# Four GpSimd scalings of the output weight behind the last normalised tile, and the stores of tiles 9 to 13 behind their adds

## The chip, the core and the metric

The kernel runs on one core of a Trainium2 chip. The core has five instruction streams that work side by side and meet only where one waits for another's semaphore: TensorE (PE, with its weight loads shown as PEld), VectorE (DVE), ScalarE (ACT), GpSimd (POOL) and SyncE (SP), which issues nearly all DMAs. The metric is device time in microseconds (us) of one execution, the median of the runs shown.

## The reference

A linear-attention mixer and a gated MLP with spatial mixing, both with adaptive layer norm from a condition vector `c`. S = 2048 rows, D = 448, 16 heads of 28, Fh = 896; all inputs are bfloat16.

```python
sa, ca, ga, sb, cb, gb = (silu(c) @ w_mod).reshape(6, -1)
h = layernorm(x) * (1 + ca) + sa
q, k, v = h @ wqkv                         # per head
phi(t) = [softmax(t @ w_phi), softmax(-t @ w_phi)]
o = (phi(q) @ (phi(k).T @ v)) / (phi(q) @ sum(phi(k)) + 1e-6)
x = x + ga * (o @ wo)
h = layernorm(x) * (1 + cb) + sb
z = gelu(h @ w_in)
z1, z2 = z[:, :Fh], layernorm(z[:, Fh:])
g = w_sp @ z2 + b_sp                       # mixes the 2048 rows
x = x + gb * ((z1 * g) @ w_out)
```

The last line is the one that the change concerns. The kernel folds `gb` into the weight: it multiplies each row block of `w_out` by `gb` once (and `wo` by `ga`), so that the product is already gated.

## The kernel before

All work is cut into tiles of 128 rows of x, numbered 0 to 15. A long string named `ORDER` (lines 482 to 525) lists every step in the order in which it is recorded, and `fast_path` (line 528) walks through it. A word such as `kP:13/G` calls the step `kP` for tile 13 on GpSimd; `/V` is VectorE, `/S` ScalarE, `/Y` SyncE; `@A0` names the PSUM bank that a matmul step writes. No scheduler moves anything afterwards: each engine executes its own instructions in the order of the string, and waits where an operand or a bank is not ready.

The stages overlap, but they come in this order. **Keys and values** (`kM`, `vM`, `kE`, `kF`, `kS`, `kR`, `kP`, `kA`): for every tile, exponentials of the key features, their sums, their normalised form (`kP`, line 873, tile `f_phik`, on VectorE or GpSimd), and an accumulation over all tiles in one bank, `kvacc`. **The joint**: when tile 15 is accumulated, `KV` and `KZ` copy `kvacc` into `f_KVbd`, and only then can the first products with the queries start. **Queries and output of the attention** (`qM`, `nM`, `nX`, `nC`, `nS`, `nT`, `nA`, `T2`, `wM`/`wN`, `wR`): `qM` (line 907) multiplies four tiles by the query weight, `qE` and `qF` exponentiate into `f_Eq`, `nM` (line 935, tile `num`) multiplies by `f_KVbd`. For a pair of tiles `nX` (ScalarE, `f_Sx`) and `nC` (VectorE, `f_cr`) prepare the denominators, `nS` is three VectorE instructions (line 950 a sum into `f_dn`, line 951 a reciprocal, line 952 a product into `f_w`), `nT` (line 955) scales a tile's numerators out of PSUM into `f_t` and so frees its bank, `nA` (line 961) adds the two halves into `f_opad` on VectorE or GpSimd, `T2` (line 834) transposes `f_opad` into `f_oT` by DMA, and `wN` (lines 969 and 971, `x_ps`) multiplies by `wo`. In between, `SHw` and `SCw` (lines 766 and 768 to 774) shift and scale the MLP's input weight `f_win`; `SCw:3,1/G` and `SCw:1,1/G` are two scalings on GpSimd that wait for `SHw:3` and `SHw:2`.

**Normalised z2** (`zM`, `zG`, `zQ`, `zR`, `zW`, `zN`) and **z1** (`yM`, `yG`) are made per tile; `zN` (line 1037, tile `f_z2n`) of tile 14 runs on GpSimd, that of tile 15 on VectorE. **Spatial mixing** (`gM`, line 1059, tile `g_ps`) multiplies `w_sp` by all sixteen tiles of `f_z2n`; `gG` (lines 1065 and 1066) adds `b_sp` and multiplies by z1. **Output** (`oM`, line 1072, `o_ps`) multiplies by `w_out`, `oE` (line 1075) adds x, and `oD` (line 1094) stores the tile. Tile 15 is done in two column parts, 256 and 192 wide: `oN` (line 1083), `oF` (line 1087), `oG` (line 1091), part 0 stored from SyncE's queue and part 1 from ScalarE's.

The two kinds of scaling that matter here share line 924: `wos:k` multiplies block k of `f_wo`, `wts:k` block k of `f_wout` (seven blocks), both 128 x 448 or 112 x 448 in bfloat16 with both inputs in SBUF. Before, `wts:4` runs early, `wts:3` late (both on GpSimd), `wts:5` on VectorE, and `wts:0`, `wts:6`, `wts:2` and `wts:1` stand on GpSimd between `kP:13` and the joint, mixed with `wos:1` to `wos:3`.

On SyncE's queue each store waits for its add; whatever stands behind it waits with it. After the last store every engine takes one branch (line 1161, to a general path that these inputs do not need) and then meets the others at the end (line 1189).

Of the kernel before, what the change touches and what calls it, by code (L numbers as in the profile page):

```python
# [498 lines left out]
T2:0,1 W:0,6 nT:1 SCw:3,1/G SCw:1,1/G SCw:0,2/V SCw:0,3/V SCw:2,1/V nA:1/G T2:1,2 qE:3 qM:4@A2 qM:5@A1 qF:4 qE:4 nM:2@A0 nM:3@A2 nX:2 nC:2 nX:3 nC:3
nS:1 qF:5 nT:2 nT:3 qE:5 wN:0@B0 wR:0/S SHw:1@B1 nM:4@A1 nM:5@A0 SCw:0,1/S nX:4 nX:5 nC:4 nC:5 nS:2 nA:2/G nT:4 nA:3/G nT:5 nA:4/G wN:1@B0 wQ:0/S  # L500
wR:1/S wQ:1/S SHw:0@B1 SCw:2,0/S l2R:0,2/G l2r:0,2 l2a:0/G SCw:0,0/V nA:5/V T2:2,4 T2:4,6 qM:6@A2 nM:6@A1 nM:7@A0 wN:2@B0 wN:3@B1 qE:6 nX:6 nC:6 nX:7
nC:7 nS:3 nT:6 nT:7 qF:6 wR:2/S wQ:2/S wR:3/S wQ:3/S l2R:2,4/V nA:6/G nA:7/G l2r:2,4 l2a:3/G l2a:2/G qM:7@A2 nM:8@A1 nM:9@A0 wN:4@B0 wM:5@B1 W:1,1
T3:0,1 T2:6,8 qE:7 nX:9 nC:9 nX:8 qF:7 zM:0@A2 wR:4/S gt zG:0 nC:8 l2a:1/V nS:4 nT:8 nT:9 T3:1,2 wR:5/V nM:10@A1 nX:10 wM:6@B0 wQ:4/V wR:6/V SCw:1,0/G
SCw:3,0/G wQ:5/S l2R:4,6/G l2r:4,6 l2a:4/G nM:11@A0 nX:11 nC:10 nC:11 zQ:0/S zM:1@A2 zG:1 zQ:1/S zR:0,2/G zW:0,2 nA:8/V nS:5 nA:9/V nT:10 T3:2,4
wM:7@B0 wR:7/V l2a:5/V W:1,5 T2:8,10 T3:4,6 yM:0,0@B1 zM:2@A2 zM:3@A1 yG:0,0 wQ:6/S zG:2 zG:3 nT:11 nM:12@A0 nM:13@A2 wQ:7/V zN:0/V zN:1/V nX:12
wM:8@B0 wM:9@B1 nC:12 nX:13 nC:13 zQ:3/S zQ:2/S zM:4@A1 nA:10/V nS:6 wR:8/V nA:11/G nT:12 nT:13 wR:9/V nA:12/V nA:13/V l2R:6,8/G l2r:6,8 l2a:6/G
l2a:7/G T2:10,12 wQ:8/S wQ:9/V zR:2,4/G zW:2,4 yM:0,1@B0 l2R:8,10/G l2r:8,10 l2a:8/G l2a:9/G zG:4 yG:0,1 zQ:4/S zN:2/V zN:3/V zM:5@A0 nM:14@A2
nM:15@A1 wN:10@B0 wN:11@B1 zG:5 nX:14 nX:15 nC:14 nC:15 nS:7 wR:10/S wQ:10/V nT:14 nT:15 nA:14/V nA:15/V wR:11/S zQ:5/S zR:4,6/G zW:4,6 T3:6,8 zM:6@A0
zG:6 wQ:11/S zQ:6/S T2:12,14 W:1,0 wM:12@B0 wM:13@B1 zM:7@A2 l2R:10,12/V yM:0,4@A1 yM:1,4@A0 l2r:10,12 l2a:11/G T3:8,10 T2:14,16 zG:7 zQ:7/S zN:4/V
zN:5/V zR:6,8/G zW:6,8 wR:13/V yG:0,4 wQ:13/S zM:8@A2 zM:9@A1 l2a:10/V wR:12/V wM:14@B0 wM:15@B1 wQ:12/V l2R:12,14/V W:1,3 T3:10,12 W:2,1 l2r:12,14  # L510
l2a:12/G zN:6/V zN:7/V yG:1,4 zG:8 zG:9 zQ:8/S W:1,4 zM:10@A2 zM:11@A1 zQ:9/S zR:8,10/G zW:8,10 zG:10 zG:11 zQ:11/S wR:14/V l2a:13/V T3:12,14 W:2,3
W:2,7 wR:15/V wQ:14/V wQ:15/V l2R:14,16/V yM:1,2@B0 zM:12@A2 zM:13@A1 yG:1,2 zG:12 yM:1,3@B0 yM:0,2@B1 yM:2,1@A2 yM:2,5@A0 zQ:10/V zN:8/V zN:9/V
zR:10,12/V l2r:14,16 l2a:14/V l2a:15/V zG:13 zQ:13/S zW:10,12 T3:14,16 W:1,2 zN:10/V zN:11/V zQ:12/V W:2,0 W:2,6 W:1,7 W:2,5 W:2,4 W:2,2 yG:1,3 yG:2,1
zM:14@A1 zM:15@A2 yG:2,5 W:1,6 zG:14 zG:15 zQ:15/S yM:1,5@B0 yG:0,2 yM:3,0@A1 yM:0,6@A2 yM:1,1@A0 yG:3,0 yG:1,1 yG:1,5 wts:3/G zR:12,14/V zW:12,14
# [679 lines left out]
```

## Time and profile before

| | us |
|---|---|
| runs: median of 3 | 263.35 |
| runs: lowest, highest | 263.28, 263.9 |
| the profiled execution's own time | 262.58 |
| its span, first instruction to last | 260.8 |
| PE busy in the span | 251.4 |
| DVE busy | 158.8 |
| ACT busy | 108.1 |
| POOL busy | 88.7 |

The profile is of one execution. Its span starts at 0 with the first instruction; 1.8 us of the execution's own time lie outside of it. Views that the text uses: the page's engine sums; busy time by stretches; the chain of waits, which is followed back from the last instruction; the timeline of an engine, where a row gives start, length, engine, line, operation, output<-inputs, how many instructions are merged in it, and in brackets how long the engine stood idle before and what ended that; and the rows of one source line. An engine's name with a q (SPq, ACTq) is its queue of instructions that issue, wait or branch. Names such as `f_win` are tiles.

### The profile page before, as it was taken

Reading aid. Unit: us, or ns where it says so; the run is one execution under the profiler, and the core shown is the slowest. Engines: PE = TensorE matmul, PEld = TensorE weight load, DVE = VectorE, ACT = ScalarE, POOL = GpSimd, SP = SyncE. Lnnn points to the kernel's source line nnn. Section 1 sums busy time; section 2 is a strip of 40 time slices with the busy share of each in tenths; the row PEclk is TensorE's granted clock in tenths of the full one; section 3 lists DMA queues with packets and bytes.
Section 4 is the critical chain, followed back from the end, with each engine's and each line's share of the span. In section 5 each row is a group of like instructions: output and inputs, shape, how many; then the busy total and the mean of one; then the engine's idle time right before and its main releaser. Section 6 shows DMA issues by size and latency. Waiting matters only on the chain.

```text
span 260.8 us, 4348 instructions
## 1 busy us (share of the span) xinstructions
PE 251.4 (96%) x1634; PEld 135.3 (52%) x1643; DVE 158.8 (61%) x358; ACT 108.1 (41%) x224; POOL 88.7 (34%) x149
## 2 busy tenths in 40 slices
PE   7999999999899999999999999999999999999992
PEld 5745655664555554444444444444444444566691
DVE  4899999869999998883005242422570283306762
ACT  3898977645899889887610400200000000000000
POOL 6419896994588887643200000000000000000000
PEclk9999999999999999999999999999999999999999
DMA  7996969993376566969600000002009700030012
GB/s 173 275 296 129 216 131 222 234 221 63 58 125 120 105 129 132 180 125 182 120 0 3 1 0 0 20 11 67 0 3 172 127 0 3 18 106 0 3 38 64
DMA packets 68799, 25.23 MB, mean 97 GB/s; under 512 B 58273, under 2 KB 68642, under 8 KB 68770
## 3 DMA queue, kind: packets, MB, share of 16 engines
q1 hardware_dynamic: 68160, 24.40, 45.6%
q10 hardware_dynamic: 610, 0.47, 0.6%
q8 instruction: 15, 0.25, 0.4%
q14 instruction: 14, 0.11, 0.2%
HBM read 8.87 MB, written 1.84 MB: 41 GB/s over the span
## 4 chain that ended last, share of the span: by engine, by line
PE 84%; DVE 9%; DMA 2%; ACT 2%; issue 1%; POOL 1%; SPq 0%; ACTq 0%; DVEq 0%
PE g_ps L1059 37%; PE z_ps L1015 9%; PE z_ps L1043 9%; PE o_ps L1072 8%; PE x_ps L971 4%; PE v_ps L860 3%; PE q_ps L907 3%; PE k_ps L852 3%; DVE f_t L955 2%; PE kvacc L883 2%; DMA f_wk_raw<-in_A_wqkv_dram 2%; PE num L935 2%; DVE f_ksum L866 2%; DVE f_phik L873 1%; PE sh_ps L761 1%
## 5 line engine op out<-in xcount | busy, mean ns | idle before, releaser
L1059 PEld LDWEIGHTS <-f_z2n 128*128 128x128 bf16 x560 | 50.1, 98 | 47.0
L1065 DVE TENSOR_TENSOR f_gb<-g_ps,f_bsp 128x512 f32<-128x512 f32 (+2 forms) x35 | 20.4, 582 | 55.9 <-PE g_ps L1059 53.7
L1059 PE MATMUL g_ps<-f_Eq,f_z2n 128*128 128x512 bf16 x218 | 49.0, 379 | 0.3
L1046 ACT ACTIVATE f_z1T<-z_ps 128x512 bf16<-128x512 f32 x28 | 15.6, 592 | 61.8 <-PE z_ps L1043 61.7
L1015 PE MATMUL z_ps<-f_win,f_hT 112*128 112x448 bf16 (+1 forms) x128 | 26.2, 352 | 0.2 <-ACT f_z2g L1019 0.2
L1043 PE MATMUL z_ps<-f_hT,f_win 113*128 113x512 bf16 (+1 forms) x112 | 26.1, 379 | 0.0
L1059 PE MATMUL g_ps<-f_hT,f_z2n 128*128 128x384 bf16 (+1 forms) x224 | 25.1, 273 | 0.0
L1059 PE MATMUL g_ps<-f_wsp,f_z2n 128*128 128x512 bf16 x109 | 24.5, 379 | 0.2
L1072 PE MATMUL o_ps<-f_wout,f_z1T 128*128 128x448 bf16 x105 | 21.7, 352 | 0.1
L1066 DVE TENSOR_TENSOR f_z1T<-f_gb,f_z1T 128x512 bf16<-128x512 f32 (+2 forms) x35 | 20.5, 585 | 1.5
L1075 DVE TENSOR_TENSOR f_xpad<-o_ps,f_x 128x448 bf16<-128x448 f32 x15 | 9.0, 619 | 20.0 <-PE o_ps L1072 20.0
L1015 PEld LDWEIGHTS <-f_hT 112*128 112x128 bf16 (+1 forms) x128 | 12.2, 97 | 12.9 <-DMA f_hT<-f_xpad 1.5
L912 ACT ACTIVATE f_Eq<-q_ps 112x1024 bf16<-112x1024 f32 x16 | 16.1, 1027 | 5.1 <-PE q_ps L907 5.0
L855 ACT ACTIVATE f_E<-k_ps 128x448 bf16<-128x448 f32 x32 | 15.9, 550 | 4.3 <-PE k_ps L852 2.5
L1043 PEld LDWEIGHTS <-f_win 113*128 113x128 bf16 (+1 forms) x112 | 10.9, 97 | 13.0
L866 DVE TENSOR_REDUCE f_ksum<-f_E 128x32 f32<-128x896 bf16 x16 | 16.7, 1060 | 0.7 <-ACT f_E L855 0.7
L955 DVE TENSOR_TENSOR f_t<-num,f_w 128x896 bf16<-128x896 f32 x16 | 16.9, 1085 | 0.4
L1019 ACT ACTIVATE f_z2g<-z_ps 128x896 bf16<-128x896 f32 x16 | 14.7, 917 | 4.3 <-PE z_ps L1015 3.9
L907 PE MATMUL q_ps<-f_hT,f_Wq 113*128 113x512 bf16 (+1 forms) x64 | 15.2, 379 | 0.6 <-DVE f_t L955 0.6
L1072 PEld LDWEIGHTS <-f_z1T 128*128 128x128 bf16 x105 | 10.2, 98 | 9.5
L860 PE MATMUL v_ps<-f_wv,f_hT 113*128 113x448 bf16 (+1 forms) x64 | 14.6, 352 | 0.0
L852 PE MATMUL k_ps<-f_Wk,f_hT 113*128 113x448 bf16 (+1 forms) x64 | 14.4, 352 | 0.0
(166 smaller groups left out, 346.6 us busy)
## 6 DMA issues: line engine op xcount, KB each, us to landing
...
```

The source lines that it names most:

```text
L852: nc.tensor.matmul(t[:, 0, 0:D], lhsT=hT[0:KR[m], i, m, :], rhs=Wk[0:KR[m], m, :], start=(m == 0), stop=(m == KC - 1))
L860: nc.tensor.matmul(t[:, 0, 0:D], lhsT=hT[0:KR[m], i, m, :], rhs=wv[0:KR[m], m, :], start=(m == 0), stop=(m == KC - 1))
L866: nc.vector.tensor_reduce(out=ksum[:, i], in_=Er[i % NR][:].rearrange("p s (c f h) -> p (s c) h f", c=4, h=HP), axis=AX.X, op=ALU.add)
L907: nc.tensor.matmul(t[:, u, :], lhsT=Wq[0:KR[m], m, cc * CB:cc * CB + P], rhs=hT[0:KR[m], 4 * st:4 * st + 4, m, :], start=(m == 0), stop=(m ...
L912: nc.scalar.activation(out=Eq[st // 2][0:CB, 2 * c2:2 * c2 + 2, s, (st % 2) * 512:(st % 2 + 1) * 512], in_=ps["q" + str(n)][0:CB, :, :], f ...
L955: nc.vector.tensor_tensor(out=tr[i % 2][:], in0=numv(i)[:, :, :, 0:DH], in1=wr[i // 2 % 2][:, i % 2].unsqueeze(3).to_broadcast([P, 2, H, D ...
L1015: nc.tensor.matmul(t[:, hf, 0:D], lhsT=hT[0:KR[m], i, m, :], rhs=win_s[0:KR[m], m, FH + hf * D:FH + (hf + 1) * D], start=(m == 0), stop=(m ...
L1043: nc.tensor.matmul(t[:, 0, :], lhsT=win_s[0:KR[m], m, fc * P:(fc + 1) * P], rhs=hT[0:KR[m], 4 * st:4 * st + 4, m, :], start=(m == 0), stop ...
L1059: nc.tensor.matmul(g[:, 0, 0:b - a], lhsT=later["z2n"][:, s_, fc * P:(fc + 1) * P], rhs=wspT[t][:, s_, a:b], start=(s_ == 0), stop=(s_ == ...
L1065: nc.vector.tensor_tensor(out=gb, in0=ps["G%d_%d" % (ch, fc)][:, 0, 0:b - a], in1=bsp[:, t * TCHF + a:t * TCHF + b], op=ALU.add)
L1066: nc.vector.tensor_tensor(out=z, in0=gb, in1=z, op=ALU.mult)
L1072: nc.tensor.matmul(ps["o" + str(t)][:, 0, 0:D], lhsT=later["z1T"][:, fc, t * P:(t + 1) * P], rhs=wout_s[:, fc, :], start=(fc == 0), stop=( ...
```

## The change

Only the string `ORDER` is edited. `wts:0/G wts:6/G wts:2/G wts:1/G` leave their places between `kE:14` and `kA:11` and stand behind `zN:14/G`, the last tile that GpSimd normalises. The three `wos` stay. The store `oD:9` moves from behind `oE:13` to behind `oE:12`; `oD:11` and `oD:12` move there too, from the end of the string, `oD:13` behind `oE:13` and `oD:14` behind `oE:14`; `oG:15,0` is written ahead of `oF:15,1`. No step is added, removed or given to another engine. The string is wrapped anew, so that most of its lines differ; the lines with moved words are:

```diff
@@ -493,35 +493,35 @@
...
-kE:13 kS:12 kR:12 kP:12/G kS:13 kR:13 kP:13/G vM:11@B0 vC:11 kA:10@A0 kM:14@B1 kE:14 kF:14 wts:0/G wos:1/G wts:6/G wos:2/G wts:2/G wts:1/G wos:3/G
-kA:11@A0 kS:14 kR:14 kP:14/V vM:12@B0 kM:15@A2 vC:12 kF:15 kE:15 vM:13@B1 vC:13 kA:12@A0 kS:15 kR:15 kP:15/V vM:14@B0 kA:13@A0 vM:15@B1 vC:14 vC:15
+kE:13 kS:12 kR:12 kP:12/G kS:13 kR:13 kP:13/G vM:11@B0 vC:11 kA:10@A0 kM:14@B1 kE:14 kF:14 wos:1/G wos:2/G wos:3/G kA:11@A0 kS:14 kR:14 kP:14/V
+vM:12@B0 kM:15@A2 vC:12 kF:15 kE:15 vM:13@B1 vC:13 kA:12@A0 kS:15 kR:15 kP:15/V vM:14@B0 kA:13@A0 vM:15@B1 vC:14 vC:15 kA:14@A0 csB@B0 kA:15@A0 esB
...
-zW:14,16 zN:14/G zN:15/V gM:0,6@B1 gM:0,3@B0 gG:0,3 gM:0,4@A2 gG:0,6 gM:0,2@B0 yM:2,4@B1 yM:2,6@A1 yG:2,6 yG:2,4 gG:0,4 gG:0,2 yM:3,5@A2 yM:3,1@B0
+yM:1,6@B0 yG:0,3 yG:1,6 yM:1,0@A0 yG:1,0 yG:3,6 yM:3,3@A1 yM:0,5@B0 yG:0,5 yG:3,3 yG:0,6 zR:14,16/V zW:14,16 zN:14/G wts:0/G wts:6/G wts:2/G wts:1/G
+zN:15/V gM:0,6@B1 gM:0,3@B0 gG:0,3 gM:0,4@A2 gG:0,6 gM:0,2@B0 yM:2,4@B1 yM:2,6@A1 yG:2,6 yG:2,4 gG:0,4 gG:0,2 yM:3,5@A2 yM:3,1@B0 yM:2,3@B1 yG:3,5
...
-gM:3,1@B1 gG:3,1 gG:3,2 gM:3,6@A0 gM:3,4@B1 gG:3,6 gG:3,4 gG:3,3 gG:3,5 oD:7/Y gM:3,0@A1 oM:11,0,7@B1 gM:4,2@B0 oD:4/Y gG:3,0 oM:12,0,7@A2 oE:11 oE:12
-oM:13,0,7@B1 oE:13 gG:4,2 oD:9/Y gM:4,6@A2 gM:4,4@A1 gM:4,3@B0 gM:4,0@B1 gG:4,4 gG:4,3 gG:4,0 gM:4,1@A1 gM:4,5@B0 hint oM:14,0,7@B1 gG:4,1 gG:4,6
-gG:4,5 oN:15,0@B0 oN:15,1@A1 oE:14 oF:15,0 oF:15,1 oD:12/Y oD:13/Y oD:14/Y oD:11/Y oG:15,0/Y oG:15,1/S
+gM:3,6@A0 gM:3,4@B1 gG:3,6 gG:3,4 gG:3,3 gG:3,5 oD:7/Y gM:3,0@A1 oM:11,0,7@B1 gM:4,2@B0 oD:4/Y gG:3,0 oM:12,0,7@A2 oE:11 oE:12 oD:9/Y oD:11/Y oD:12/Y
+oM:13,0,7@B1 oE:13 oD:13/Y gG:4,2 gM:4,6@A2 gM:4,4@A1 gM:4,3@B0 gM:4,0@B1 gG:4,4 gG:4,3 gG:4,0 gM:4,1@A1 gM:4,5@B0 hint oM:14,0,7@B1 gG:4,1 gG:4,6
+gG:4,5 oN:15,0@B0 oN:15,1@A1 oE:14 oD:14/Y oF:15,0 oG:15,0/Y oF:15,1 oG:15,1/S
```

What this makes of the engines' own orders is shown by rows of line, operation, output<-inputs, shape and, where it is printed, what the instruction waits for. The first place is GpSimd at the joint; a minus stands before and a plus in the changed kernel. Line 873 is `kP` of tiles 12 and 13, line 772 the two scalings of `f_win`, line 961 `nA:1`.

```order
 L873 TENSOR_TENSOR f_phik<-f_E_127,f_kr_133 128x896
 L873 TENSOR_TENSOR f_phik<-f_E_128,f_kr_134 128x896
-L924 TENSOR_TENSOR f_wout<-f_wout,f_g_rep 128x448
-L924 TENSOR_TENSOR f_wo<-f_wo,f_g_rep 112x448
-L924 TENSOR_TENSOR f_wout<-f_wout,f_g_rep 128x448
-L924 TENSOR_TENSOR f_wo<-f_wo,f_g_rep 112x448
-L924 TENSOR_TENSOR f_wout<-f_wout,f_g_rep 128x448 x2
-L924 TENSOR_TENSOR f_wo<-f_wo,f_g_rep 112x448
+L924 TENSOR_TENSOR f_wo<-f_wo,f_g_rep 112x448 x3
 L772 TENSOR_SCALAR f_win<-f_win,f_cb_81 112x896 x2
 L961 TENSOR_TENSOR f_opad<-f_t_109 128x4x112
```

Seven instructions between `kP:13` and the scalings of `f_win` have become three.

The second place is GpSimd's last work in the changed kernel; the row of line 1106 is the read of a flag that ends its program.

```order
L1037 TENSOR_SCALAR f_z2n<-f_z2g_1268,f_zm,f_zv 128x896
L1001 TENSOR_TENSOR f_zv<-f_zv,f_mhalf 128x2
L1037 TENSOR_SCALAR f_z2n<-f_z2g_1269,f_zm,f_zv 128x896
L924 TENSOR_TENSOR f_wout<-f_wout,f_g_rep 128x448 x4
L1106 TENSOR_LOAD flag
L1161 COMPARE_AND_BRANCH
```

The four moved scalings stand behind `zN:14` (the second row of line 1037), where before the flag's read followed at once.

The third place is the end of SyncE's queue. Before, the four rows of line 1094 are the stores of tiles 12, 13, 14 and 11, and line 1091 is part 0 of tile 15; DVE_49 is a wait for VectorE, DMAHW a wait for an earlier DMA of the same semaphore.

```order
L1094 DMA out_dram<-f_xpad 128x448 [waits DMAHW1_49,DVE_49]
L1094 DMA out_dram<-f_xpad 128x448 [waits DMAHW2_49,DVE_49]
L1094 DMA out_dram<-f_xpad 128x448 [waits DMAHW3_49,DVE_49]
L1094 DMA out_dram<-f_xpad 128x448 [waits DMAHW4_49]
L1091 DMA out_dram<-f_xpad 128x256 [waits DMAHW5_49,DVE_49]
```

In the changed kernel the same five places read:

```order
L1094 DMA out_dram<-f_xpad 128x448 [waits DMAHW1_49,DVE_49]
L1094 DMA out_dram<-f_xpad 128x448 [waits DMAHW2_49,DVE_49]
L1094 DMA out_dram<-f_xpad 128x448 [waits DMAHW3_49,DVE_49]
L1094 DMA out_dram<-f_xpad 128x448 [waits DMAHW4_49,DVE_49]
L1091 DMA out_dram<-f_xpad 128x256 [waits DMAHW5_49,DVE_49]
```

They are now tiles 11, 12, 13 and 14, each with a wait of its own for VectorE. The store of tile 11, which before waited for nothing more than its place behind that of tile 14, no longer stands between tile 14 and the first part of tile 15. PE, VectorE and ScalarE keep their orders.

More of the change, by code (lines that the diff above doesn't have):

```diff
@@ L499 @@
[L499 to L514, printed above, removed]
@@ new lines @@
+yM:3,2@A2 yG:3,4 yG:2,0 yG:3,2 guard@A0 gM:1,5@B1 oM:1,0,7@A2 oE:1 oE:2 oE:3 gM:1,2@A0 gG:1,2 gM:1,1@B0 gM:1,3@A2 gM:1,0@A1 gG:1,3 gG:1,0 gM:1,6@A2
+oD:0/Y oD:3/Y oD:2/Y gG:1,1 gG:1,5 gG:1,6 gM:2,0@B0 yM:2,2@B1 yG:2,2 W:3,0 W:3,3 W:3,7 W:3,1 W:3,6 W:3,4 W:3,2 gM:2,2@A2 gG:2,0 oM:6,0,7@B0 gM:2,3@B1
+oM:4,0,7@A1 gM:2,5@A0 oE:4 gG:2,5 gG:2,3 gM:2,6@A1 gG:2,6 gG:2,2 oM:5,0,7@B1 oE:5 oE:6 gM:2,4@A0 gM:2,1@B0 gG:2,1 oM:7,0,7@B1 oE:7 W:3,5 oD:1/Y
+gM:3,3@A2 read gG:2,4 oM:8,0,7@B0 oE:8 oM:10,0,7@B1 oM:9,0,7@B0 oE:9 oE:10 oD:8/Y oD:10/Y oD:6/Y oD:5/Y gM:3,2@A1 gM:3,5@B0 gM:3,1@B1 gG:3,1 gG:3,2
```

25 lines of the change are left out of this document (18 added, 7 removed).

## The prediction

> **What bounds the kernel now.** The page's engine sums and chain come first, then the busy time by stretches (us from the start of the span; busy time and number of instructions of each engine, granted clock, DMA).
>
> ```profile
> span 260.8 us, 4348 instructions
> PE 251.4 (96%) x1634; PEld 135.3 (52%) x1643; DVE 158.8 (61%) x358; ACT 108.1 (41%) x224; POOL 88.7 (34%) x149
> ...
> PE 84%; DVE 9%; DMA 2%; ACT 2%; issue 1%; POOL 1%; SPq 0%; ACTq 0%; DVEq 0%
> ...
> 57.00:71.00 14.00, 12.66 (x91) 6.61 (x89) 13.39 (x25) 10.14 (x22) 7.14 (x8) 1.00 0.33 69
> 71.00:112.00 41.00, 40.77 (x261) 21.80 (x262) 37.49 (x108) 36.96 (x89) 33.62 (x74) 1.00 0.72 131
> 112.00:130.00 18.00, 17.95 (x88) 8.36 (x87) 7.60 (x23) 13.19 (x27) 5.92 (x7) 1.00 0.78 142
> 130.00:162.00 32.00, 31.89 (x147) 14.46 (x149) 9.89 (x15) 3.99 (x8) 0.00 (x0) 1.00 0.00 1
> ```
>
> PE ends last: 96% busy, 84% of the chain. From 71 to 162 us it idles 0.39 us out of 91, so there nothing is won unless PE arrives earlier. The one later stretch with a sizeable hole is 57 to 71: PE misses 1.34 us there, and DVE is full (13.39 of 14). That is just behind the joint, so the chain of waits is read there (start, length, what):
>
> ```profile
> 55.97 0.88 PE num L935 x16
> ...
> 57.32 0.81 DVE f_dn L950
> ...
> 58.15 0.36 DVE f_dn L951
> ...
> 58.54 1.01 DVE f_w L952
> ...
> 59.58 1.10 DVE f_t L955
> ...
> 61.01 1.08 DVE f_t L955
> 62.10 1.54 DVE f_win L774 x3
> ...
> 70.96 0.59 PE num L935 x8
> ```
>
> From 57.32 to 70.96 the path that sets the end runs through DVE. Two pieces look wrong for their size: `f_dn` and `f_w` are 32 and 64 elements wide. The rows of their lines (min/median/max in ns over eight) say so, and GpSimd's timeline says what stood beside them:
>
> ```profile
> L950 DVE TENSOR_TENSOR f_dn<-f_cr x8: 178/192/924, 57.3 to 95.4; 128x32 f32<-128x32 f32 x8
> ...
> L952 DVE TENSOR_TENSOR f_w<-f_Sx,f_dn x8: 224/224/1003, 58.5 to 96.1; 128x64 f32<-128x64 f32 x8
> ...
> 52.67 1.44 POOL L924 TENSOR_TENSOR f_wout<-f_wout,f_g_rep 128x448 bf16<-128x448 bf16 x1
> ...
> 55.06 2.02 POOL L924 TENSOR_TENSOR f_wout<-f_wout,f_g_rep 128x448 bf16<-128x448 bf16 x2
> 57.05 1.02 POOL L924 TENSOR_TENSOR f_wo<-f_wo,f_g_rep 112x448 bf16<-112x448 bf16 x1
> 58.46 2.00 POOL L772 TENSOR_SCALAR f_win<-f_win,f_cb 112x896 bf16<-112x896 bf16 x2 [0.39 <-PE sh_ps L766]
> ```
>
> `f_dn` starts at 57.32 inside GpSimd's `wos:3` (57.05 to 58.07) and ends at 58.12; `f_w` starts at 58.54 inside the first scaling of `f_win` (58.46 to about 59.46) and ends at 59.54. Each ends within 0.1 us of GpSimd's instruction: a DVE instruction with two inputs in SBUF is held until GpSimd's current one is through. [...]
>
> **The change part by part.** (1) *The joint.* `wos:3` ends at 58.07 because four `wts` stand ahead of it. Now the three `wos` take the places of the first three rows from 50.27 on and end at about 54.1; the next GpSimd work, the scalings of `f_win`, waits for PE (0.39 idle, released by `sh_ps`) and stays at 58.46. So GpSimd is empty from 54.1 to 58.46. Ahead of 54.1 DVE finds GpSimd as busy as before, and I count nothing. Then, with the medians: `f_dn` 57.32 + 0.19; reciprocal 57.54 to 57.90; `f_w` 57.93 to 58.15, 0.3 us ahead of the scaling that caught it; `f_t` 58.19 to 59.28 instead of 60.67, 1.39 us earlier. `f_t` itself reads PSUM and one SBUF input and took 1.09 beside the second scaling, as it does everywhere, so no hold is counted for it.
>
> How much of the 1.39 reaches PE is in these rows of PE, PEld, ACT and DVE:
>
> ```profile
> 58.19 1.90 PE L907 MATMUL q_ps<-f_hT,f_Wq 113*128 113x512 bf16 x8
> 60.73 1.91 PE L907 MATMUL q_ps<-f_hT,f_Wq 113*128 113x512 bf16 x8 [0.64 <-DVE f_t L955]
> 62.47 1.00 PE L935 MATMUL num<-f_KVbd,f_Eq 112*128 112x120 bf16 x16
> ...
> 63.59 0.49 PEld L971 LDWEIGHTS <-f_oT 112*128 112x128 bf16 x4 [0.24 <-DMA f_oT<-f_opad]
> ...
> 60.12 1.94 ACT L912 ACTIVATE f_Eq<-q_ps 112x1024 bf16<-112x1024 f32 x2 [2.14 <-PE q_ps L907]
> ...
> 63.51 0.18 ACT L943 COPY f_Sx<-num 128x32 f32<-128x32 f32 x1 [0.23 <-PE num L935]
> ...
> 60.70 0.39 DVE L961 TENSOR_TENSOR f_opad<-f_t 128x448 bf16<-128x448 bf16 x1
> ...
> 63.56 0.36 DVE L946 TENSOR_TENSOR f_cr<-num,f_Sx 128x32 f32<-128x32 f32 x2
> ```
>
> The second `q_ps` waits for the bank that `f_t` frees. Eight of these matmuls pass in 1.74 us when nothing holds them (60.73 to the `num` at 62.47), so the first eight are through at 58.19 + 1.74 = 59.93, and then PE can go on. It starts at 59.93 instead of 60.73: **0.80 us** of the 1.39. `num` follows at 61.67; its second tile at 62.09 needs ACT's two exponentials, done at 60.12 + 1.94 = 62.06 as before, just in time. DVE adds `f_opad` from 59.31 (held until 59.46 by the first scaling), the next `f_t` starts at about 59.8 and the three `f_win` end at about 62.5. The second `f_Sx`, 63.51 before, comes with PE at 62.71, and `f_cr` behind it ends 0.80 earlier too. `f_oT`, which PEld waited for at 63.59, follows `f_opad` and is 1.2 us earlier, which PE no longer waits for. From here PE, ACT, DVE and GpSimd all stand 0.80 earlier relative to one another as before, until 70.96, where PE takes the chain over and carries it on. I take 0.80 to 0.87 (0.07 more where `f_oT` held PE); bounds: 1.39, if PE could use all of DVE's gain, and 0, if the hold has another cause.
>
> (2) *The new place.* Four scalings of 1.01 us (half of 2.02, the undisturbed pair above) follow `zN:14`:
>
> ```profile
> 124.45 1.31 POOL L1037 TENSOR_SCALAR f_z2n<-f_z2g,f_zm,f_zv 128x896 bf16<-128x896 bf16 x1
> ...
> 136.67 0.69 DVE L1065 TENSOR_TENSOR f_gb<-g_ps,f_bsp 128x512 f32<-128x512 f32 x1 [11.78 <-PE g_ps L1059]
> ...
> 162.40 0.92 PE L1072 MATMUL o_ps<-f_wout,f_z1T 128*128 128x448 bf16 x4
> ```
>
> They run from 125.76 to about 129.8. DVE idles for 11.78 us until 136.67, so from 124.89, and nobody meets them; `f_z2n` 14 is already done, and the first reader of `f_wout` is PE at 162.40, 32 us later. The window 130 to 162 shows GpSimd empty. Cost 0; the cover would have to shrink from 32 us to none before the four, 4.0 us together, cost anything.
>
> (3) *The stores.* SyncE's and ACT's last issues, the last adds and the branch that follows (of the last row pairs: first and last start):
>
> ```profile
> 255.26 1.16 SPq L1094 DMA_DIRECT2D out_dram<-f_xpad  x2
> 256.52 0.38 SPq L1091 DMA_DIRECT2D out_dram<-f_xpad  x1
> ...
> 256.34 0.38 ACTq L1091 DMA_DIRECT2D out_dram<-f_xpad  x1
> ...
> L1161 SPq EVENT_SEMAPHORE  x8: 17/17/17, 257.5 to 259.1; - x8
> L1161 POOLq COMPARE_BRANCH  x1: 45/45/45, 169.1 to 169.1; - x1
> L1161 POOLq EVENT_SEMAPHORE  x1: 17/17/17, 171.7 to 171.7; - x1
> ...
> L1161 ACTq COMPARE_BRANCH  x1: 54/54/54, 256.8 to 256.8; - x1
> L1161 ACTq EVENT_SEMAPHORE  x1: 17/17/17, 259.9 to 259.9; - x1
> ```
>
> Without tile 11 between them, tile 15's part 0 issues when its add allows, about 255.84 instead of 256.52: 0.68 earlier on SyncE. But ACT's store at 256.34 is untouched and becomes the last, so the last landing moves by 256.52 - 256.34 = 0.18. And SyncE has seen every store at 259.1, while ACT's first instruction behind its branch comes only at 259.9, 3.1 us after the branch: that, not a store, ends last. GpSimd's branch, with no store in flight, needed 2.6 (169.1 to 171.7). So the gain is 0 if ACT's 3.1 stands, and about 0.25 if one store less in flight shortens it. I take **0.1**. The other stores issue into an empty queue and nobody waits for them.
>
> Sum: 0.80 to 0.87 + 0 + 0.1, about 0.95 us. On the profiled execution's own 262.58 (span 260.8 and 1.8 around it) that is 261.6; this execution lay 0.77 below the median of 263.35, so the forecast is 263.35 - 0.95 = **262.4**.
>
> **The rivals.** *A, caught again.* `f_opad` on DVE, two SBUF inputs, now comes at 59.31, between GpSimd's two back-to-back scalings of `f_win` (58.46 to 60.46). If GpSimd's second takes its turn ahead of the waiting DVE, `f_opad` ends at 60.5, the `f_t` behind it at 61.6, the three `f_win` at 63.2, `f_cr` at 63.4 or 63.5 against 63.92: about 0.35 to 0.4 is left of 0.80. Against it: `f_w`, waiting from 58.54, got in as the first scaling ended. Time 263.35 - 0.4 - 0.1 = 262.85. [...]
>
> *B, the change does not do this.* `f_dn` is slow for another reason (it also has the first use of its tile), or the gain is swallowed before 70.96 by a wait that I do not see. Then only the stores count: 263.35 - 0.1, 263.2. Against it: `f_dn` at its slowest, 924 ns, is not this first one, and the later uses at the median have no GpSimd work beside them.
>
> *C, slower.* Everything behind the joint is re-timed, and from 71 to 112 DVE (37.49 of 41) and GpSimd (33.62) are both nearly full. Each new meeting of a small DVE instruction with a GpSimd one costs up to 0.924 - 0.192 = 0.73. One such is less than the gain; from the second that PE has to wait for, the time is above before; with three, 3 x 0.73 - 0.95 = +1.2, so 264.55. Against it: both engines move together, so that their meetings stay where they are, and DVE has 3.5 us of slack there while PE waits 0.23.
>
> **How the numbers follow.** Chances: forecast 0.62, A 0.16, B 0.12, C 0.10. 0.3%, 0.79 us, is about what a measurement of this kernel can tell from no change. Faster by more: four fifths of the forecast (its sum is 0.16 above the bound, and runs scatter by some tenths) and a third of A, 0.50 + 0.05 = 0.55. Slower by more: nearly all of C, 0.09. Within: 0.36. Range: from 261.8 (the joint's gain nearer its bound of 1.39, the stores' 0.25) to 263.4 (B and a little scatter), which leaves out C and some seven in a hundred at the ends. The forecast's own range is 262.0 to 262.7.
>
> **What would show it.** Right, if in the new profile `f_dn` and `f_w` at about 57 to 58 take 0.19 and 0.22, GpSimd is empty between 54.1 and 58.46, the second `q_ps` group starts at about 59.9 with no wait for `f_t`, and `g_ps` of the mixing starts near 128.7 instead of 129.5. A shows as an `f_opad` of more than 1 us at 59.3. B shows as an unchanged `f_dn`. C shows as more of the eight `f_dn` and `f_w` rows near 0.9 and as idle time of PE between 71 and 112. For the stores: ACT's instruction behind its branch against SyncE's last one. The prediction is wrong if the shift at 59.9 is there and the end is not 0.6 to 1.2 us earlier, or if it comes from elsewhere.

## The result, and the profile after

| | before | changed |
|---|---|---|
| median of the runs beside each other, us | 263.70 (22 runs) | 261.87 (22 runs) |
| lowest, highest | 261.78, 264.47 | 260.93, 263.13 |
| ratio, with its 95% interval | | 0.9940 (0.9924 to 0.9955) |
| the profiled execution's own time | 262.58 | 262.05 |

The change makes the kernel faster by about 1.6 us, 1.2 to 2.0 by the interval. (A ratio here is not the quotient of the two medians, which would be 0.9931.) The median of before is 0.35 above that of the three runs shown earlier; over more runs (35, 35 and 13) beside the experiments it came out at 263.37, 263.32 and 263.45.

The page of the changed kernel (engine sums and chain), and then busy time by the same four stretches as before:

```profile
span 260.3 us, 4358 instructions
PE 252.6 (97%) x1643; PEld 137.3 (53%) x1643; DVE 157.3 (60%) x358; ACT 108.1 (42%) x224; POOL 88.6 (34%) x149
...
PE 91%; DMA 3%; POOL 2%; ACT 1%; issue 0%; SPq 0%; DVE 0%; POOLq 0%
```

```profile
57.00:71.00 14.00, 13.19 (x103) 7.41 (x101) 12.37 (x26) 10.78 (x24) 6.21 (x6) 1.00 0.36 81
71.00:112.00 41.00, 40.67 (x262) 22.09 (x262) 37.23 (x107) 36.63 (x89) 33.19 (x73) 1.00 0.71 130
112.00:130.00 18.00, 18.00 (x88) 8.33 (x86) 7.81 (x24) 13.48 (x27) 10.08 (x11) 1.00 0.74 146
```

DVE's share of the chain falls from 9% to nothing, and DVE's busy time behind the joint from 13.39 to 12.37 us with nearly the same work (25 and 26 instructions). The scalings show up again from 112 to 130 us (POOL 10.08 instead of 5.92), where PE is as full as before.

The two executions can't be laid over each other from 0. VectorE's fifth `f_ksum` (line 866) starts here, before and after:

```profile
28.24 1.08 DVE L866 TENSOR_REDUCE f_ksum<-f_E 128x32 f32<-128x896 bf16 x1 [0.37 <-ACT f_E L855]
```

```profile
29.21 1.09 DVE L866 TENSOR_REDUCE f_ksum<-f_E 128x32 f32<-128x896 bf16 x1 [0.36 <-ACT f_E L855]
```

The changed kernel's execution is 0.97 us late by then, in code that the change doesn't touch. So every stage is measured from that row on. The joint's instructions on DVE, GpSimd's row with the new place, and PE, in the timeline of the changed kernel:

```profile
58.03 0.19 DVE L950 TENSOR_TENSOR f_dn<-f_cr 128x32 f32<-128x32 f32 x1
58.26 0.35 DVE L951 RECIPROCAL f_dn<-f_dn 128x32 f32<-128x32 f32 x1
58.64 0.22 DVE L952 TENSOR_TENSOR f_w<-f_Sx,f_dn 128x64 f32<-128x64 f32 x1
58.90 1.09 DVE L955 TENSOR_TENSOR f_t<-num,f_w 128x896 bf16<-128x896 f32 x1
60.03 0.40 DVE L961 TENSOR_TENSOR f_opad<-f_t 128x448 bf16<-128x448 bf16 x1
...
51.01 3.81 POOL L924 TENSOR_TENSOR f_wo<-f_wo,f_g_rep 112x448 bf16<-112x448 bf16 x3
59.17 2.13 POOL L772 TENSOR_SCALAR f_win<-f_win,f_cb 112x896 bf16<-112x896 bf16 x2 [4.36 <-PE sh_ps L766]
...
125.54 3.99 POOL L924 TENSOR_TENSOR f_wout<-f_wout,f_g_rep 128x448 bf16<-128x448 bf16 x4
...
58.90 3.63 PE L907 MATMUL q_ps<-f_hT,f_Wq 113*128 113x512 bf16 x16
...
78.00 1.69 PE L1015 MATMUL z_ps<-f_win,f_hT 113*128 113x448 bf16 x8 [0.33 <-DMA f_hT<-f_xpad]
```

`f_dn` and `f_w` take 0.19 and 0.22 us (0.80 and 1.00 before), GpSimd is idle for 4.36 us ahead of the `f_win` scalings, and all sixteen `q_ps` run in one row with no wait for `f_t`. A new wait stands at 78.00, for the DMA transpose of `f_hT`. Whether an execution pays it varies: PE idles 0.33 us there in this one, 0.70 in a second one of the same kernel (e5 below), and not at all in that of before. The next table lays the executions side by side, stage by stage (us; every start and end is that of one instruction: the fifth `f_ksum`, the first `KV` copy on line 893, the second group of eight `q_ps`, the first `o_ps` on line 1072, the end of the last add on line 1087, the end of the span):

| kernel | f_ksum to KV | KV to 2nd q_ps | q_ps to o_ps | o_ps to last add | last add to end | sum |
|---|---|---|---|---|---|---|
| before | 25.66 | 6.83 | 101.67 | 93.92 | 4.47 | 232.55 |
| changed | 25.40 | 6.02 | 101.56 | 93.92 | 4.14 | 231.04 |
| changed, again (e5) | 25.35 | 6.03 | 102.40 | 93.92 | 4.06 | 231.76 |

Between the first two rows the joint gives 0.81, the end 0.33, the stage ahead of the joint 0.26 and the stretch behind it 0.11: 1.51 us. Of the 0.26, 0.23 can be seen in a single `f_phik` at 37 to 38 us, which took 1.02 in before and 0.79 here (more on that place under e2). The same kernel a second time loses 0.84 of the gain between `q_ps` and `o_ps`.

The end of the program, rows of lines 1161 and 1189 and SyncE's and ACT's last stores in the changed kernel:

```profile
255.63 0.56 SPq L1091 DMA_DIRECT2D out_dram<-f_xpad  x1
...
256.15 0.38 ACTq L1091 DMA_DIRECT2D out_dram<-f_xpad  x1
...
L1161 SPq EVENT_SEMAPHORE  x8: 17/17/17, 256.8 to 258.6; - x8
...
L1161 ACTq COMPARE_BRANCH  x1: 54/54/54, 256.6 to 256.6; - x1
...
L1161 ACTq EVENT_SEMAPHORE  x1: 17/17/17, 259.4 to 259.4; - x1
...
L1189 SPq EVENT_SEMAPHORE  x10: 17/28/333, 258.6 to 260.2; - x10
```

Tile 15's part 0 issues at 255.63 instead of 256.52. SyncE has seen all stores at 258.6, then goes through eight more waits on line 1189 of 28 ns each (spaced by 0.06), and the last of them lasts 333 ns, because it waits for ACT's first instruction behind its branch.

### The profile page after: what moved, and what is told of

It is laid out like the page before. It is cut to its first block, busy times and chain, and to the rows that moved or that the text cites. A ratio compares the mean times of both kernels' runs of the same rounds, so it can differ in the third digit from the quotient of the medians.

```text
span 260.3 us, 4358 instructions
## 1 busy us (share of the span) xinstructions
PE 252.6 (97%) x1643; PEld 137.3 (53%) x1643; DVE 157.3 (60%) x358; ACT 108.1 (42%) x224; POOL 88.6 (34%) x149
## 4 chain that ended last, share of the span: by engine, by line
PE 91%; DMA 3%; POOL 2%; ACT 1%; issue 0%; SPq 0%; DVE 0%; POOLq 0%
PE g_ps L1059 37%; PE z_ps L1015 9%; PE z_ps L1043 9%; PE o_ps L1072 8%; PE q_ps L907 5%; PE v_ps L860 4%; PE k_ps L852 4%; PE x_ps L971 3%; PE kvacc L883 3%; PE num L935 2%; DMA f_wq_raw<-in_A_wqkv_dram 2%; PE tps L795 1%; ACT f_Eq L912 1%; DMA f_hT<-f_xpad 1%; PE sh_ps L761 1%; PE sh_ps L766 1%
```

## The experiments

Medians beside those of before on the same chip; the ratio stands with its 95% interval. In the diffs, words of `ORDER`. The first four share a median of 263.37 for before (35 runs).

**e1, the scalings alone.** Stores as before.

```diff
-kF:14 wts:0/G wos:1/G wts:6/G wos:2/G wts:2/G wts:1/G wos:3/G kA:11@A0
+kF:14 wos:1/G wos:2/G wos:3/G kA:11@A0
-zN:14/G zN:15/V
+zN:14/G wts:0/G wts:6/G wts:2/G wts:1/G zN:15/V
```

> Only the four scalings move; the stores stay as before. Theory (the hold of f_dn and f_w at the joint): these two take 0.19 and 0.22 us, PE's second q_ps group starts 0.8 us earlier against the start of the joint, and the time is 0.8 to 0.95 us below before (ratio 0.9964 to 0.997). Rival (the stores bring the most): less than 0.4 us below before, ratio above 0.9985.

262.78 us, ratio 0.9978 (0.9958 to 0.9999). In its trace the joint is that of the whole change: KV to `q_ps` 6.02, `f_dn` 0.19, `f_w` 0.23. Its end is that of before, and shows what the forecast had missed:

```profile
L1161 ACTq EVENT_SEMAPHORE  x1: 17/17/17, 259.2 to 259.2; - x1
...
L1189 SPq EVENT_SEMAPHORE  x10: 17/28/28, 259.0 to 260.3; - x10
```

No wait of SyncE on line 1189 is longer than 28 ns: ACT's instruction behind its branch came at 259.2, before SyncE was through, and the program ended behind the last store and SyncE's eight waits. From the last add to the end it took 4.56 us.

**e2, the stores alone.** All four scalings stay at the joint.

```diff
-oE:11 oE:12 oM:13,0,7@B1 oE:13 gG:4,2 oD:9/Y
+oE:11 oE:12 oD:9/Y oD:11/Y oD:12/Y oM:13,0,7@B1 oE:13 oD:13/Y gG:4,2
-oE:14 oF:15,0 oF:15,1 oD:12/Y oD:13/Y oD:14/Y oD:11/Y oG:15,0/Y oG:15,1/S
+oE:14 oD:14/Y oF:15,0 oG:15,0/Y oF:15,1 oG:15,1/S
```

> Only the stores move; the four scalings stay at the joint. Theory: the joint is as before (f_dn 0.80, f_w 1.00), and only the last microseconds change, by 0.1 us as forecast or by 0.33 us as the changed kernel's trace has it (ratio 0.9987 to 0.9996). Rival (the stores bring the most): 0.6 us or more, ratio below 0.9977.

262.85 us, ratio 0.9980 (0.9961 to 0.9999); last add to end 4.34. The surprise stands at the joint, in the timeline of DVE and GpSimd:

```profile
58.85 0.19 DVE L950 TENSOR_TENSOR f_dn<-f_cr 128x32 f32<-128x32 f32 x1
...
59.47 0.23 DVE L952 TENSOR_TENSOR f_w<-f_Sx,f_dn 128x64 f32<-128x64 f32 x1
...
57.58 1.03 POOL L924 TENSOR_TENSOR f_wo<-f_wo,f_g_rep 112x448 bf16<-112x448 bf16 x1
60.00 1.01 POOL L772 TENSOR_SCALAR f_win<-f_win,f_cb 112x896 bf16<-112x896 bf16 x1 [1.38 <-PE sh_ps L766]
```

With the same seven scalings at the joint, `wos:3` ends at 58.61 and `f_dn` comes at 58.85, 0.24 later: nothing is held. In this execution the `KV` copy itself is later beside GpSimd (f_ksum to KV 25.83, against 25.35 to 25.53 in the profiles of the change, e1 and e4 to e6). The fork is at 38 us, in the stage ahead. DVE and GpSimd of the changed kernel (before is like it), and then of e2:

```profile
38.27 2.16 DVE L873 TENSOR_TENSOR f_phik<-f_E,f_kr 128x896 bf16<-128x896 bf16 x2
...
35.78 2.80 POOL L829 TENSOR_SCALAR f_xpad<-f_x,f_nm,f_rs 128x448 bf16<-128x448 bf16 x4
38.55 1.39 POOL L924 TENSOR_TENSOR f_wo<-f_wo,f_g_rep 112x448 bf16<-112x448 bf16 x1
```

```profile
38.59 1.14 DVE L873 TENSOR_TENSOR f_phik<-f_E,f_kr 128x896 bf16<-128x896 bf16 x2
...
36.58 3.65 POOL L829 TENSOR_SCALAR f_xpad<-f_x,f_nm,f_rs 128x448 bf16<-128x448 bf16 x4
40.20 1.02 POOL L924 TENSOR_TENSOR f_wo<-f_wo,f_g_rep 112x448 bf16<-112x448 bf16 x1
```

Either `wos:0` gets in between DVE's two `f_phik`, and these take 2.16 us together; or both `f_phik` pass first (1.14) and GpSimd's fourth `f_xpad` waits for them (the four take 3.65 instead of 2.80). From there on the two engines alternate in another order. Below, the first of these orders is called the phase of the change, the second the phase of e2. In the four profiles of the second kind (e2, e3, e8, e9) the fourth `f_xpad` starts 0.02 to 0.10 us behind the first of the two `f_phik`; in nine others it starts 0.16 to 0.41 ahead of it.

**e3, one scaling moved.** Only `wts:1` goes behind `zN:14`; the stores are those of before.

> Only wts:1 moves behind zN:14; wts:0, wts:6 and wts:2 stay at the joint and the stores stay as before. GpSimd's row of scalings then ends at about 57.05 on the clock of the profile before, 0.27 us ahead of f_dn at 57.32. Theory (a hold by whatever instruction GpSimd is in): f_dn and f_w are free and the whole gain of the four is there, 0.8 to 0.95 us (ratio 0.9964 to 0.997). Rival (DVE is slowed by GpSimd's work in proportion to it): a quarter of it, 0.2 us (ratio 0.999).

262.86 us, ratio 0.9977 (0.9956 to 0.9998). Its profiled execution is in the phase of e2 (f_ksum to KV 25.94), and as in e2 nothing is held: `f_dn` 0.19 and `f_w` 0.23; last add to end 4.50. By the medians one scaling moved is as good as four, which fits a meeting that is there or not, but in that phase the trace can't show it.

**e4, the scalings left out.** The four `wts` are nowhere, so four blocks of `f_wout` stay without their factor; stores as before.

> wts:0, wts:6, wts:2 and wts:1 are left out altogether, so that four of the seven row blocks of w_out are not gated; the stores stay as before. Theory (the new place costs nothing): the time is that of the run that moves only the scalings, within 0.2 us. Rival (the four cost something behind zN:14, by what they share with PE or ACT there): 0.3 us or more below that run.

262.69 us, ratio 0.9962 (0.9939 to 0.9984). By the medians that is 0.09 us below e1, by the ratios (e1 has 0.9978) about 0.4, and the two intervals overlap: the times alone don't exclude the rival's 0.3 us. That the new place costs nothing is read from the trace of the change: the four end at 129.53, PE is busy for all of the 18 us from 112 to 130, and the first `o_ps`, which reads `f_wout`, comes at 162.2. KV to `q_ps` is 6.02 here.

The next four share a median of 263.32 for before (35 runs).

**e5, the whole change again.**

> The whole change once more, beside fresh runs of the kernel before. Theory 'the parts add up': the scalings alone gave a ratio of 0.9978 and the stores alone 0.9980, so together about 0.9958, 262.2 to 262.5 us if before is near 263.4. Rival 'the first comparison was right and the parts help each other': 0.994, about 261.8. In the trace, under both: the first f_dn about 0.19 and f_w about 0.22, and PE's second q_ps group 6.0 us behind the first KV copy. If the hold at the joint comes and goes with the execution's phase also here, f_dn would be above 0.5 in this one.

262.17 us, ratio 0.9947 (0.9926 to 0.9968). The parts alone multiply to 0.9978 x 0.9980 = 0.9958, inside this interval and just above the first one's upper end of 0.9955. That fits two parts that add up; the intervals are too wide to exclude that one helps the other. `f_dn` 0.19 and 6.03 us from KV to `q_ps`.

**e6, the new wait at 78 us.** `W:1,1`, a transpose of w_sp on SyncE's queue, stands behind `T3:0,1` (line 1009) instead of ahead of it.

```diff
-wM:5@B1 W:1,1 T3:0,1 T2:6,8
+wM:5@B1 T3:0,1 W:1,1 T2:6,8
```

> The change, and on SyncE's queue the weight load W:1,1 stands behind the transpose T3:0,1 instead of ahead of it. Theory 'T3 is late because of what stands ahead of it': PE's wait for T3 at 78 us (0.49 in the changed kernel's profile, 0.12 before) falls below 0.15 and T3:0,1 issues about 1.2 us earlier; time 0.2 to 0.5 below the change's. Rival 'another wait takes its place': the 0.49 shows up again at one of the next places (f_hT of the next tile, f_z2g at 111 us) and the time stays within 0.1 of the change's.

262.72 us, ratio 0.9978 (0.9958 to 0.9998): 0.55 above e5, whose median it was to undercut. PE's timeline:

```profile
78.46 1.69 PE L1015 MATMUL z_ps<-f_win,f_hT 113*128 113x448 bf16 x8
80.15 0.59 PE L935 MATMUL num<-f_KVbd,f_Eq 112*128 112x120 bf16 x8
81.70 0.93 PE L971 MATMUL x_ps<-f_wo,f_oT 112*128 112x448 bf16 x4 [0.95 <-DMA f_oT<-f_opad]
```

`z_ps` no longer waits, but the next transpose, `f_oT`, is late by 0.95, since `W:1,1` now stands ahead of that one. The rival holds in what becomes of the wait: it moves on along the queue. Between `q_ps` and `o_ps`, where the edit acts, this profile takes 102.50 us against 102.40 in e5. In time the rival asked for 0.1, and the medians are 0.55 apart, with intervals that overlap. (PE's timeline of the change has 0.33 for the wait that the expectation puts at 0.49, and none in before for its 0.12.)

**e7, e6 and one hold less.** Also the add `nA:3` on VectorE ahead of `nT:4`, so that GpSimd doesn't hold the third `f_dn` (0.93 in the changed kernel).

```diff
-nS:2 nA:2/G nT:4 nA:3/G nT:5
+nS:2 nA:2/G nA:3/V nT:4 nT:5
```

> The change, the W load behind T3 as in the run beside it, and in the attention stage the add nA:3 on VectorE instead of GpSimd, ahead of nT:4, so that GpSimd does not hold the third f_dn there (0.92 in before, 0.93 in after). Theory 'each hold that PE's next wait sees costs': third f_dn about 0.19, PE's wait of 0.56 at 70.9 us falls by 0.2 to 0.3, time 0.4 to 0.8 below the change's. Rival 'VectorE is full there': the added 0.4 us on VectorE eats the 0.73 that the hold costs and GpSimd's next add holds another one; time within 0.2 of the run beside it.

261.89 us, ratio 0.9947 (0.9924 to 0.9969), the same ratio as e5. The third `f_dn` takes 0.19. That hold is gone, but a new one has come: the fifth `f_w` takes 0.53 instead of 0.22, beside an `f_xpad` of GpSimd. The time is that of the change. Neither sentence of the expectation fits it: it was to be 0.4 to 0.8 below the change, or within 0.2 of e6, and it is 0.28 below e5 and 0.83 below e6, by medians whose ratios overlap.

**e8, memsets at the joint.** The scalings behind `zN:14` as in the change, stores as before, and behind `wos:3` four memsets of an unused tile on GpSimd (the new function moves line numbers above 923 up by 3).

```diff
-kF:14 wts:0/G wos:1/G wts:6/G wos:2/G wts:2/G wts:1/G wos:3/G kA:11@A0
+kF:14 wos:1/G wos:2/G wos:3/G fill:0 fill:1 fill:2 fill:3 kA:11@A0
+    def fill(n):
+        nc.gpsimd.memset(junk[:], 0.0)
```

> Stores as in before; the four scalings behind zN:14 as in the change; in their place at the joint GpSimd has four memsets of an unused tile behind the three wos, which read nothing from SBUF. Everything of the reference is computed. Theory 'it is any GpSimd instruction that holds VectorE's two-input ones': f_dn and f_w that meet a memset take up to the rest of it, f_phik at 50 to 54 us are held as in before, time as before, 263.2 to 263.5. Rival 'only a GpSimd instruction that reads two inputs in SBUF holds': f_dn, f_w and f_phik at their medians (0.19, 0.22, 0.2 to 0.3), PE's second q_ps group 6.0 us behind the first KV copy, time as with the scalings moved alone, 262.6 to 262.9.

262.38 us, ratio 0.9965 (0.9944 to 0.9986). It decides nothing on its question: the memsets end at 57.58, `f_dn` comes at 58.68, and no VectorE instruction with two inputs in SBUF starts beside one. It is in the phase of e2 too (f_ksum to KV 25.92), without the scalings.

The last four share a median of 263.45 for before (13 runs). e9 and e10 are one execution each, since their verdict rests on rows.

**e9 and e10, the disputed cost by itself.** The change, with GpSimd kept busy from 54 to 60 us: by six multiplications (e9), or by seven memsets as in e8 (e10). The lines of the joint are 3 higher in both.

```diff
-kF:14 wos:1/G wos:2/G wos:3/G kA:11@A0
+kF:14 wos:1/G wos:2/G wos:3/G load:0 load:1 load:2 load:3 load:4 load:5 kA:11@A0
+    def load(n):
+        nc.gpsimd.tensor_tensor(out=junk[:, 0:D], in0=wout_s[:, 0, :], in1=g_rep[:, 1, :], op=ALU.mult)
```

> The change, and at the joint GpSimd has six extra multiplications of the scalings' kind behind wos:3 (two inputs in SBUF, 128x448, their product goes to a tile that nobody reads; everything of the reference is computed). At 1.02 us each they fill GpSimd from 54 to 60 us. Theory 'a VectorE instruction with two inputs in SBUF is held by GpSimd's': the first f_dn and f_w are held, 0.5 to 1.1 us each, and f_opad behind f_t too; PE's second q_ps group 0.4 to 1.0 later behind the KV copy than the 6.02 of the change. Rival 'f_dn and f_w were slow for another reason (first use of their tiles, the place in the program)': 0.19 and 0.22 as in the change.

> As the run beside it, with seven memsets (128x896, 0.84 us each in the run before, no input) in place of the six multiplications; GpSimd is again full from 54 to 60 us. Everything of the reference is computed. Theory 'any GpSimd instruction holds': f_dn and f_w 0.4 to 0.9 each. Rival 'only GpSimd instructions that read SBUF hold': f_dn 0.19, f_w 0.22, q_ps 6.02 behind the KV copy.

DVE and GpSimd in e9:

```profile
59.17 0.19 DVE L953 TENSOR_TENSOR f_dn<-f_cr 128x32 f32<-128x32 f32 x1
...
59.78 0.70 DVE L955 TENSOR_TENSOR f_w<-f_Sx,f_dn 128x64 f32<-128x64 f32 x1
...
61.65 0.98 DVE L964 TENSOR_TENSOR f_opad<-f_t 128x448 bf16<-128x448 bf16 x1
...
58.26 1.04 POOL L924 TENSOR_TENSOR f_junk<-f_wout,f_g_rep 128x448 bf16<-128x448 bf16 x1
...
59.38 1.03 POOL L924 TENSOR_TENSOR f_junk<-f_wout,f_g_rep 128x448 bf16<-128x448 bf16 x1
```

and in e10:

```profile
57.93 0.19 DVE L953 TENSOR_TENSOR f_dn<-f_cr 128x32 f32<-128x32 f32 x1
...
58.54 0.22 DVE L955 TENSOR_TENSOR f_w<-f_Sx,f_dn 128x64 f32<-128x64 f32 x1
...
57.36 0.84 POOL L924 MEMSET f_junk<- 128x896 bf16 x1
...
58.26 0.84 POOL L924 MEMSET f_junk<- 128x896 bf16 x1
```

In e9 `f_w` starts inside a multiplication that ends at 60.41 and ends 0.08 us behind it; `f_opad` (0.40 undisturbed) is held to 0.98 by a scaling of `f_win`. `f_dn` starts only 0.13 ahead of the end of a multiplication and loses nothing, so a hold of `f_dn` was expected and not seen.

The 0.48 that `f_w` lost do not reach PE either: `f_t` ended 5.86 us behind the `KV` copy, in time for the `q_ps` group at 6.03, where a delay of 0.4 to 1.0 was expected. The forecast has room for that: by its working 0.59 of the 1.39 us that `f_t` would gain was not to reach PE. The larger cost is ahead of the joint: f_ksum to KV took 26.83, against 25.40 in the change. About half a microsecond of that is the phase of e2, in which this execution is (25.83 to 25.94 in e2, e3 and e8); the rest comes with one `f_phik` of DVE that took 1.87. Time 264.64 beside 263.45, one run.

In e10 `f_dn` starts 0.57 into a memset, 0.27 ahead of its end, and `f_w` 0.28 into the next, and they take 0.19 and 0.22. Beside these memsets, which read nothing from SBUF, neither was held; beside a multiplication of e9, which reads two tiles, `f_w` took 0.70. No semaphore stands between the two engines here (the row of `f_w` in e9 has no idle time ahead of it), so that the description of the core ahead of the prediction, in which engines meet only at semaphores, is too simple. Time 262.62, one run.

Not every GpSimd instruction that reads SBUF held `f_w`, though. In the timeline of before the fifth `f_w` and GpSimd stand like this; the two `f_xpad` have 448 elements a partition, and the first ends at 78.43:

```profile
77.78 0.23 DVE L952 TENSOR_TENSOR f_w<-f_Sx,f_dn 128x64 f32<-128x64 f32 x1
...
77.67 1.46 POOL L1004 TENSOR_SCALAR f_xpad<-f_x,f_m,f_v 128x448 bf16<-128x448 bf16 x2
```

`f_w` starts 0.11 us into `f_xpad` and isn't held. In e7 and e12, where it starts 0.25 and 0.27 into it, it takes 0.53 and 0.51. And beside GpSimd's work on `f_v`, two elements wide and up to 0.93 us long, `f_dn` and `f_w` keep to between 0.18 and 0.23 in all fourteen profiles. So the holds of `f_dn` and `f_w` given here (0.51 to 1.00 us) stand beside GpSimd instructions of 448 or 896 elements a partition, and not every such instruction holds them. Where the limit lies isn't shown: the first `f_w` of before was held (1.00) from 0.08 us into a scaling.

**e11, wos:0 out of the fork.** The change, and `wos:0` behind `wos:3`.

```diff
-T1:12,14 wos:0/G kF:8
+T1:12,14 kF:8
-wos:3/G kA:11@A0
+wos:3/G wos:0/G kA:11@A0
```

> The change, and wos:0, which GpSimd runs at 37 to 40 us beside VectorE's f_phik, moved behind wos:3. In seven of the ten profiles so far wos:0 took 1.40 and held an f_phik of VectorE to 1.45; in the other three VectorE won and the KV copy came with f_phik of 0.85 to 0.88 and a wait of PE of 0.33 to 0.37 for it. Theory 'wos:0 decides the phase of the stage and costs there': no f_phik above 1.1 at 37 to 40 us, the first KV copy 0.3 to 0.8 earlier behind the stage's start, time 0.2 to 0.6 below the change's. Rival 'PE sets the pace of that stage': f_phik shorter, the KV copy where it was, time within 0.2 of the change's.

262.29 us, ratio 0.9955 (0.9936 to 0.9974). The fork is gone, and another `f_phik` is held in its place, by the `wos` further on (DVE's timeline):

```profile
38.49 1.30 DVE L873 TENSOR_TENSOR f_phik<-f_E,f_kr 128x896 bf16<-128x896 bf16 x2
...
50.44 1.46 DVE L873 TENSOR_TENSOR f_phik<-f_E,f_kr 128x896 bf16<-128x896 bf16 x1
```

f_ksum to KV is 25.50, with PE waiting 0.77 for that `f_phik`. The rival comes nearer: the copy is where it was; but it is the next hold that keeps it there.

**e12, the third hold alone.** The change, and `nA:3` on VectorE as in e7.

> The change and only the add nA:3 on VectorE ahead of nT:4, the W load where the change has it. Theory 'the third hold costs the time that PE waits for f_t at 70.9 us': third f_dn 0.19, PE's wait there at most 0.3 instead of 0.56, time 0.2 to 0.4 below the change's, about 261.6 beside a before of 263.4. Rival 'what PE gains here it waits for the transposes at 76 to 79 us': the wait for f_oT or f_hT there grows by what the first one shrinks, time within 0.2 of the change's.

261.69 us, ratio 0.9940 (0.9922 to 0.9957). The third `f_dn` and PE:

```profile
L950 DVE TENSOR_TENSOR f_dn<-f_cr x8: 182/191/206, 57.2 to 94.2; 128x32 f32<-128x32 f32 x8
```

```profile
70.54 0.93 PE L971 MATMUL x_ps<-f_wo,f_oT 112*128 112x448 bf16 x4 [0.32 <-DMA f_oT<-f_opad]
```

None of the eight `f_dn` is held any more, and PE's wait for `f_t` at 70.9 us has gone, but PE now waits 0.32 at 70.54, for a transpose. The fifth `f_w` is held instead, 0.51, as in e7. Which of the two sentences of the expectation is right stays open. 261.69 beside 263.45 is what the theory gave, but the ratio is that of the change (0.9940, and 0.9947 in e5), and the change didn't run beside it. In its one profile PE's waits don't grow further on, as the rival has it: `q_ps` to `o_ps` takes 101.27, against 101.56 and 102.40 in the two of the change. No kernel here beats the change beyond its interval.

## Why the prediction was right, point by point

**The number**: 261.87 is 0.07 us inside the lower end of the range (261.8) and 0.13 below the 262.0 to 262.7 that the forecast gave as its own. The gain forecast was 0.95 us, the measured one 1.2 to 2.0. That the range held it is partly luck: its lower end was put there for a joint that gives more than 0.80, and in the trace the joint gave 0.81. The stores gave more than was allowed for, and the rest is not accounted for.

**What bounds the kernel**: right. PE still ends last, its chain share went from 84% to 91%, and the 1.34 us that it missed from 57 to 71 us shrank to 0.81.

**The joint (0.80 to 0.87)**: the mechanism is shown. With the scalings gone, `f_dn` took 0.19 and `f_w` 0.22 or 0.23 in all seven executions that have only the three `wos` there, and e9 beside e10 shows for `f_w` that what GpSimd runs beside it makes the difference (0.70 beside a multiplication that reads two tiles, 0.22 beside a memset that reads none), not the place in the program. The forecast's sentence that GpSimd's current instruction holds such a VectorE one until it is through is too wide: beside the memsets of e10 (0.19 and 0.22) and the `f_xpad` of before at 77.67 (0.23) nothing was held. `f_dn` was held at the joint in one profile alone, that of before; but the third `f_dn` is held by GpSimd's add in twelve of the fourteen (0.62 to 0.93), and takes 0.19 in the two that move this add away (e7, e12). The 0.81 from KV to `q_ps` is the forecast's 0.80. Two things were not seen. First, the hold at the joint shows only in one of two phases: in e2 and e3 the scalings stood there and nothing was held, while the `KV` copy came 0.3 to 0.6 later than in those of the change, e1 and e4 (25.83 and 25.94 against 25.35 to 25.50). Like must be compared with like here. In the phase of the change, `f_ksum` to `q_ps` took 32.49 with the scalings (before) and 31.38 to 31.61 without (the two of the change, e1, e4, e6, e7, e12): 0.9 to 1.1 us of gain. In the phase of e2 it took 31.85 and 31.96 with the scalings (e2, e3) and 31.95 without them (e8, with memsets in their place): none. How often an execution of before falls into which phase, no run tells. Second, part of the gain goes to the transposes behind. The forecast has PE, ACT, DVE and GpSimd move on together by 0.80, and leaves out SyncE's queue: SyncE issues the transpose of `f_hT` 21.02 us behind the `KV` copy in before, and 20.74 and 20.88 in the two of the change, only 0.28 and 0.14 earlier. `q_ps` to `o_ps` took 101.67 in before; in the change, e1, e4 and e5 it took 101.56, 102.08, 102.57 and 102.40, so that three of these four gave back 0.4 to 0.9. That the medians of e1 show 0.59 (0.03 to 1.1 by the interval), not 0.8, agrees with both.

**The new place (0)**: right by the trace. The four run in one row from 125.54 to 129.53, where PE has no hole. e1 against e4 gives 0.09 by the medians and 0.4 by the ratios, neither clear of the intervals.

**The stores (0.1)**: this is the term that was mis-sized, at the step "that, not a store, ends last". In before's profile ACT's instruction behind its branch came 3.13 us after it, the longest of all fourteen profiles (2.62 to 3.06 in the others), and so hid that SyncE, after its last store, has eight more waits to go: it ended only 0.30 ahead. In the other four profiles with the old stores (e1, e3, e4, e8) SyncE ended last, with every wait on line 1189 at 28 ns; in the nine with the new ones it always waited there for ACT, 159 to 616 ns. From the last add to the end the five took 4.47 to 4.68, mean 4.57, the nine 3.96 to 4.40, mean 4.19: **0.38 us**. e2's median gives 0.52 (0.03 to 1.0). The forecast's 0.18 for the last landing was read from an unusually early one: it came 2.64 us behind the last add in before, 2.97 to 3.15 in the other four with the old stores, and 2.29 to 2.66 in the nine. And the other way in which the stores might have gained, a shorter 3.1 of ACT, isn't what happened: from ACT's branch to its next instruction it took 2.93 in the mean of the five and 2.85 in that of the nine.

So the sum by what was measured is 0.59 + 0.38, about 1.0, from the single parts (1.1 with e2's median), against 0.95 forecast and 1.2 to 2.0 and 0.8 to 2.0 in the two comparisons of the whole change. What made the first comparison come out at 1.6 is not accounted for beyond that; its median of before, 263.70, is 0.25 to 0.38 above the three others. By the forecast's own test the end should come 0.6 to 1.2 us earlier: the first pair of profiles fails it with 1.51, of which 0.26 lies ahead of the joint and 0.23 is the stores' error; the second profile passes it with 0.79. The forecast of 262.4 was made from a median of 263.35; from 263.70 it would have been 262.75.

**Rival A** did not happen: `f_opad` took 0.40 at 60.03. It got in as the first `f_win` scaling ended, and GpSimd's second waited for it: the two took 2.13 instead of 2.00. (In its working, 63.92 less 63.4 or 63.5 is 0.5 or 0.4, not 0.35 to 0.4.) **Rival B** is refuted by `f_dn` at 0.19. Its counter-argument, that the later uses at the median have no GpSimd work beside them, is misread: in before five of these six run beside GpSimd instructions, all of them two elements wide. **Rival C**, new meetings, showed none among the eight `f_dn` and `f_w` rows except the third `f_dn`, which was held before as well (0.92, then 0.93). The new wait that did come was of a kind that no rival named, the transpose of `f_hT`: 0.33 of PE's idle time at 78.00, which the execution of the change made up for by 111 us, where before waited 0.23 for `f_z2g`. A new meeting of the kind of C does show in e7 and e12, where the fifth `f_w` is held (0.53 and 0.51).
